# Fused attention and two MLPs: Q and K stored with a head's columns as rows

## The chip, the core and the metric

One NeuronCore of a Trainium2 chip runs the whole program. The metric is device time in microseconds (us) of one execution, given as the median of several. Engines are named as in the profile: PE is TensorE (matmuls; PEld its weight loads), DVE is VectorE, ACT is ScalarE, POOL is GpSimd, SP is SyncE, from whose queue nearly all transfers are issued.

## The reference

Eight batches of eight heads with 576 tokens and 64 columns a head. Keys and values are averaged over groups of 8 tokens (72 pooled rows a head), attention runs over the pooled rows, and its output (4608 tokens x 512) goes through two MLPs one after the other:

```python
k_p = k.reshape(B, H, Sp, pool, D).mean(axis=3)
v_p = v.reshape(B, H, Sp, pool, D).mean(axis=3)
scores = scale * np.matmul(q, k_p.transpose(0, 1, 3, 2))
attn = softmax(scores)
x = np.matmul(attn, v_p)          # then laid out as tokens x 512
h = x @ w_in;  x = (h - np.tanh(h)) @ w_out       # 512 -> 2048 -> 512
h = x @ w2_in; out = (h * np.cos(h)) @ w2_out     # 512 -> 2048 -> 512
```

Q, K and V are 32-bit floats; the MLP weights come as 64-bit floats, which the kernel reads as pairs of 32-bit words and splits into a high and a low part (three matmuls for each product).

## The kernel before, in words

Tokens are worked in blocks of 512 (nine blocks). For each block the first MLP runs 16 steps over slices of 128 hidden columns: `emit_h` (L590, 12 matmuls of 128x512 into PSUM tile `h`), the nonlinearity on ACT and DVE (L600 to L618), and two steps later `emit_out1` (L625, 12 matmuls into `acc`). The second MLP follows (L911 and L990), in an order written out by hand. Block 0 also converts the first MLP's weights as they arrive (`converter`, L173 to L193), blocks 1 to 7 those of the second.

Attention for the tokens of the coming blocks is spread between these steps. It works on tiles of 128 or 96 tokens (five a batch) and is cut into *items*, of which `slot` takes a share ahead of each step; each item's loads are issued `LOOK = 4` items before the item itself. For a batch:

- `load_k` (L260) brings K as five chunks of 128 pooled rows (the last has 64), each row with its 8 tokens of 64 columns; `pool_kv` adds them up on DVE in three halving steps (L291, L291, L292) into `kp`; for batch 0 it is one reduction (L287). ACT doubles the sums (L295).
- `kprep`, in two parts of three and two chunks, transposes `kp` on PE (L325) and lets ACT copy the result into `bd`, a block diagonal of two heads a chunk: 128 rows (two heads' columns) by 144 (two heads' pooled rows), by L332, L336 and L341.
- `load_q` (L346) brings a tile of Q with tokens as rows, in pieces of 64 numbers; `s1` transposes it on PE (L355, four a tile) and ACT copies it to `qT` (L357).
- `s2` multiplies `qT` by `bd` (L371, four matmuls in two halves), takes the maxima (L374), subtracts (L378) and exponentiates (L380); `norm` sums and divides (L385 to L388); `s3` transposes the weights (L400, L410); `pv` multiplies by the pooled V (L433) and writes the MLP's input (L436, L440).

V goes the same way as before and after the change. Up to the first `emit_h` (L1089 to L1188) the order is written out by hand under `manual_schedule`, with `spin` (L1141) for dummy transpositions; there V is summed on POOL. In blocks 0 to 7 the framework's scheduler may reorder what the program lists; from block 8 on the listed order holds. `att_tile` hands out the PSUM tiles of the attention, two in turn.

Of the kernel before, what the change touches and what calls it, by code (L numbers as in the profile page):

```python
# [8 lines left out]
F32 = mybir.dt.float32  # L9
# [31 lines left out]
def fused_kernel(ctx: ExitStack, tc: tile.TileContext, q, k, v, w1i, w1o, w2i, w2o, out):  # L41
    nc = tc.nc
    B, H, S, D = q.shape
    NT, DM = out.shape
    DFF = w1i.shape[1]
# [12 lines left out]
    NKC = (H * SP + 127) // 128  # L58
# [83 lines left out]
    def src_of(wi, wo, f, s):  # L142
        if s == 0:
            return wi.bitcast(U32)[:, f * 256:(f + 1) * 256].rearrange("(c p) n -> p c n", p=128)
        return wo.bitcast(U32)[f * 128:(f + 1) * 128, :]

    def raw_load(src, pool=None, tag="raw"):
        raw = (pool or ap).tile([128, 1024], U32, tag=tag, name="raw", bufs=2)
        nc.sync.dma_start(out=raw.rearrange("p (c n) -> p c n", c=KC) if len(src.shape) == 3 else raw, in_=src)
        return raw  # L150
# [72 lines left out]
    kp = ap.tile([128, NKC, 128], F32, name="kp")  # L223
# [3 lines left out]
    bd = ap.tile([128, NP, 2 * SP], F32, name="bd")  # L227
# [9 lines left out]
    KSPLIT = ((0, 3), (3, NKC))  # L237
# [19 lines left out]
    def load_k(b, c, pool=None, tag="kv", bufs=4):  # L257
        n = min(128, H * SP - c * 128)
        t = slab(tag) if tag in PLACES else (pool or ap).tile([128, POOL * D], F32, tag=tag, name="kv", bufs=bufs)
        nc.sync.dma_start(out=t[:n], in_=k[b].rearrange("h (s r) d -> (h s) (r d)", r=POOL)[c * 128:c * 128 + n, :])  # L260
        raw_kv["k", b, c] = t

    def load_v(b, c, pool=None, tag="kv", bufs=4):
        t = slab(tag) if tag in PLACES else (pool or ap).tile([128, POOL * D], F32, tag=tag, name="kv", bufs=bufs)
# [11 lines left out]
    def pool_kv(which, b, c):  # L276
        t = raw_kv.pop((which, b, c))
        if which == "k":
            n = min(128, H * SP - c * 128)
            o = kp[:n, c, 0:D]  # L280
        elif c < NP:
# [4 lines left out]
        if b == 0 and which == "k":  # L286
            nc.vector.tensor_reduce(o, t[:n].rearrange("p (r d) -> p d r", r=POOL), axis=AX.X, op=ALU.add)  # L287
        else:
            engine = nc.vector if b else nc.gpsimd
            for w in (POOL * D // 2, POOL * D // 4):  # L290
                engine.tensor_tensor(t[:n, :w], t[:n, :w], t[:n, w:2 * w], op=ALU.add)  # L291
            engine.tensor_tensor(o, t[:n, :D], t[:n, D:2 * D], op=ALU.add)  # L292
        if which == "k" and (c == NKC - 1 or (b == 0 and c == KSPLIT[0][1] - 1)):
            c0 = (KSPLIT[1][0] if c == NKC - 1 else 0) if b == 0 else 0
            nc.scalar.activation(out=kp[:, c0:c + 1, D:2 * D], in_=kp[:, c0:c + 1, 0:D], func=AF.Copy)  # L295
# [23 lines left out]
    def kprep(part):  # L319
        c0, c1 = KSPLIT[part]  # L320
        at = att_tile()
        lo, hi = c0 * 128, min(c1 * 128, H * SP)
        for c in range(c0, c1):
            n = min(128, H * SP - c * 128)
            nc.tensor.transpose(at[:, (c - c0) * 128:(c - c0) * 128 + n], kp[:n, c, :], ident[:n, :n])  # L325
        for e in range(2):
            p = e * D
            whole = [h for h in range(e, H, 2) if h * SP >= lo and (h + 1) * SP <= hi]
            m = len(whole)
            x = whole[0] * SP - lo if m else 0  # L330
            if m > 1:
                nc.scalar.activation(  # L332
                    out=bd[p:p + D, whole[0] // 2:whole[0] // 2 + m, e * SP:(e + 1) * SP],
                    in_=at[p:p + D, x:x + 2 * m * SP].rearrange("p (m t) -> p m t", m=m)[:, :, 0:SP], func=AF.Copy)
            elif m:
                nc.scalar.activation(out=bd[p:p + D, whole[0] // 2, e * SP:(e + 1) * SP], in_=at[p:p + D, x:x + SP], func=AF.Copy)  # L336
            for h in range(e, H, 2):
                x0, x1 = max(h * SP, lo), min((h + 1) * SP, hi)
                if h not in whole and x0 < x1:
                    o = e * SP + x0 - h * SP  # L340
                    nc.scalar.activation(out=bd[p:p + D, h // 2, o:o + x1 - x0], in_=at[p:p + D, x0 - lo:x1 - lo], func=AF.Copy)  # L341

    def load_q(t, pool=None, tag="qt", bufs=2, queue=None):
        n = t["n"]
        qt = (pool or ap).tile([128, H * D], F32, tag=tag, name="qt", bufs=bufs)
        (queue or nc.sync).dma_start(  # L346
            out=qt[:n].rearrange("p (h d) -> p h d", h=H),
            in_=q[t["b"], :, t["s"]:t["s"] + n, :].rearrange("h s d -> s h d"))
        t["qt"] = qt

    def s1(t):
        n, qt = t["n"], t.pop("qt")
        at = att_tile()
        for p in range(NP):
            nc.tensor.transpose(at[:, p * 128:p * 128 + n], qt[:n, p * 128:(p + 1) * 128], ident[:n, :n])  # L355
        qT = ap.tile([128, NP, 128], F32, tag="qT", name="qT", bufs=2)
        nc.scalar.activation(out=qT[:, :, :n], in_=at.rearrange("p (g n) -> p g n", g=NP)[:, :, :n], func=AF.Copy)  # L357
        t["qT"] = qT
# [113 lines left out]
    def start_q(t):  # L472
        item(lambda: s1(t), lambda: load_q(t))
# [7 lines left out]
    item(lambda t=t: s1(t), lambda t=t: load_q(t))  # L481
# [7 lines left out]
    item(lambda: None)
    post_kv("k", 1, 4)  # L490
    item(lambda: kprep(0), apart=True)
    post(lambda t=t: norm(t))
    post_kv("v", 1, 0)
    item(lambda t=t: s3(t, 0))
    post_kv("v", 1, 1)
    item(lambda: kprep(1))
    post_kv("v", 1, 2)
    item(lambda t=t: s3(t, 1))
    post_kv("v", 1, 3)
    start_q(tiles[n1])  # L500
    post_kv("v", 1, 4)
# [18 lines left out]
    for c in range(NKC):  # L520
        item(lambda: None)
        post_kv("k", 2, c)
        post_kv("v", 2, c)
    post_kv("v", 2, 5)
    post(lambda: place_v(2))
    item(lambda: kprep(0))
    item(lambda: kprep(1))
    start_q(tiles[n2])

    for ti in range(n2, len(tiles)):  # L530
        t = tiles[ti]
# [551 lines left out]
    if True:  # L1083
# [5 lines left out]
        with tc.manual_schedule():  # L1089
# [16 lines left out]
            load_q(tiles[2], cp, "xe", 4, nc.scalar)  # L1106
            load_q(tiles[3], cp, "xe", 4, nc.scalar)
# [177 lines left out]
```

## Time and profile before

| what | value |
|---|---|
| median of 3 runs | 1728.77 us (1727.46 to 1730.01) |
| the profiled execution, its own time | 1728.11 us |
| its span, first to last instruction | 1726.3 us |
| PE busy | 1696.8 us (98%) |
| PEld, DVE, ACT, POOL busy | 1450.8, 1448.3, 1158.8, 13.8 us |
| mean granted TensorE clock | 0.996 of full speed |
| moved by DMA | 280.24 MB, mean 162 GB/s |

The profile shows one execution. A group of instructions is given with its line, engine, output and input, count, busy time, mean length, and the idle time of the engine just before it with what ended most of that. Matmuls overlap in time, so a group's busy time is more than the time by which it delays what follows; starts tell that. The span leaves out about 2 us of the execution's own time around it.

### The profile page before, as it was taken

How to read it: one execution, taken by the hardware profiler on the slowest of the kernel's cores; microseconds unless marked ns; L12 is line 12 of the kernel's file. 1: busy time of each engine (PE TensorE's matmuls, PEld its weight loads, DVE VectorE, ACT ScalarE, POOL GpSimd, SP SyncE). 2: the span in 40 equal slices, each digit the busy share in tenths (PEclk: the TensorE clock that was granted, in tenths of full speed). 3: DMA queues.
4: the chain of work that ended last, by engine and by line, in shares of the span. 5: the costliest groups of instructions: out<-in, count | busy, mean ns of one | idle time of the engine just before them, and what ended most of it. 6: DMA issues, size and time to landing. Idle time of an engine off the chain costs nothing.

```text
span 1726.3 us, 24077 instructions
## 1 busy us (share of the span) xinstructions
PE 1696.8 (98%) x8268; PEld 1450.8 (84%) x8268; DVE 1448.3 (84%) x2535; ACT 1158.8 (67%) x1926; POOL 13.8 (1%) x30
## 2 busy tenths in 40 slices
PE   6999999999999999999999999999999999999998
PEld 4767888888888888888888888999999998999997
DVE  7899998879999898888767687887887888888776
ACT  5787767767777776776666565656656666656655
POOL 2000000000000000000000000000000000000000
PEclk9999999999999999999999999999999999999999
DMA  7566545556565654636366663532542632632430
GB/s 241 187 213 231 182 139 173 179 183 203 185 224 175 217 184 149 203 134 197 132 205 233 220 198 97 174 114 86 178 127 70 200 111 79 191 120 78 148 98 37
DMA packets 162105, 280.24 MB, mean 162 GB/s; under 512 B 50112, under 2 KB 69568, under 8 KB 161984
## 3 DMA queue, kind: packets, MB, share of 16 engines
q1 hardware_dynamic: 157824, 277.66, 50.2%
q10 hardware_dynamic: 4160, 1.05, 0.3%
q8 instruction: 66, 1.08, 0.2%
q14 instruction: 55, 0.45, 0.1%
HBM read 228.33 MB, written 50.33 MB: 161 GB/s over the span
## 4 chain that ended last, share of the span: by engine, by line
PE 92%; DVE 3%; ACT 3%; DMA 1%; issue 1%; SPq 0%; ACTq 0%
PE acc L990 22%; PE h L590 22%; PE acc L625 22%; PE ab L911 20%; PE att L433 2%; PE att L371 2%; PE att L400 1%; PE att L355 1%; DMA raw<-in_moe_w_in_dram 1%; PE att L410 0%; DMA kv<-in_k_dram 0%; DVE tmp L956 0%; DVE tmp L955 0%; PE att L325 0%; PE acc L433 0%
## 5 line engine op out<-in xcount | busy, mean ns | idle before, releaser
L990 PE MATMUL acc<-wo,gh 128*128 128x512 f32 x1152 | 356.8, 391 | 0.4 <-ACT gh L974 0.4
L911 PE MATMUL ab<-xh,ws 128*128 128x384 f32 x952 | 258.3, 336 | 2.0 <-DVE hB L925 1.4
L990 PEld LDWEIGHTS acc<-wo,gh 128*128 128x128 f32 x1152 | 214.9, 188 | 41.4 <-ACT gh L974 0.8
L990 PE MATMUL acc<-wo,gl 128*128 128x512 f32 x576 | 226.2, 393 | 0.3 <-DVE gl L978 0.3
L590 PE MATMUL h<-xh,wi 128*128 128x512 f32 x576 | 197.1, 401 | 0.1
L590 PE MATMUL h<-xh,ri 128*128 128x512 f32 x576 | 196.5, 401 | 0.0
L625 PE MATMUL acc<-gh,wo 128*128 128x512 f32 x576 | 179.9, 395 | 4.6 <-ACT gh L617 4.6
L625 PE MATMUL acc<-gh,ro 128*128 128x512 f32 x576 | 178.7, 392 | 1.2 <-ACT gh L617 1.2
L911 PEld LDWEIGHTS ab<-xh,ws 128*128 128x128 f32 x952 | 173.5, 188 | 5.9 <-DVE hB L925 2.1
L606 DVE SCALAR_TENSOR_TENSOR tmp<-tmp,h 128x512 f32<-128x512 f32 x144 | 98.4, 683 | 83.2 <-ACT tmp L601 82.4
L911 PE MATMUL ab<-xl,ws 128*128 128x384 f32 x476 | 159.6, 335 | 0.0
L600 ACT ACTIVATE tmp<-h 128x512 f32<-128x512 f32 x144 | 85.5, 594 | 74.5 <-PE h L590 73.9
L617 ACT ACTIVATE gh<-tmp 128x512 fp32r<-128x512 f32 x144 | 90.9, 631 | 62.1 <-DVE tmp L611 59.8
L625 PEld LDWEIGHTS acc<-gh,wo 128*128 128x128 f32 x576 | 108.4, 189 | 28.3 <-ACT gh L617 6.1
L625 PEld LDWEIGHTS acc<-gh,ro 128*128 128x128 f32 x576 | 108.4, 189 | 24.0 <-ACT gh L617 1.5
L990 PEld LDWEIGHTS acc<-wo,gl 128*128 128x128 f32 x576 | 108.0, 188 | 23.6 <-DVE gl L978 0.8
L590 PEld LDWEIGHTS h<-xh,ri 128*128 128x128 f32 x576 | 108.1, 188 | 22.9 <-DVE ri L178 0.9
L974 ACT ACTIVATE gh<-tmp 128x768 fp32r<-128x768 f32 x96 | 81.3, 847 | 67.8 <-DVE tmp L969 67.8
L590 PEld LDWEIGHTS h<-xh,wi 128*128 128x128 f32 x576 | 108.0, 188 | 22.1 <-DVE wi L178 0.6
L609 ACT ACTIVATE tmp<-tmp,bias_m 128x512 f32<-128x512 f32 x144 | 104.1, 723 | 30.9 <-DVE tmp L606 30.3
L922 ACT ACTIVATE z<-ab 128x384 f32<-128x384 f32 x48 | 23.5, 490 | 143.3 <-PE ab L911 143.3
L611 DVE COPY_PREDICATED tmp<-tmp 128x512 f32<-128x512 uint32 x144 | 108.5, 754 | 8.8 <-ACT tmp L609 0.5
(208 smaller groups left out, 3620.3 us busy)
## 6 DMA issues: line engine op xcount, KB each, us to landing
ws<-s2i SPq DMA_DIRECT2D x294, 256.0 KB, 3.0
ri<-s1i SPq DMA_DIRECT2D x64, 512.0 KB, 3.9
ro<-s1o SPq DMA_DIRECT2D x64, 512.0 KB, 3.6
raw<-in_moe_w_in_dram SPq DMA_DIRECT2D x32, 512.0 KB, 4.1
raw<-in_moe_w_out_dram SPq DMA_DIRECT2D x32, 512.0 KB, 3.5
x1s<-xe SPq DMA_DIRECT2D x36, 256.0 KB, 4.1
wo<-s2o SPq DMA_DIRECT2D x18, 512.0 KB, 5.4
out_dram<-xe SPq DMA_DIRECT2D x36, 256.0 KB, 4.1
```

What stands on the lines that cost most here:

```text
L371: nc.tensor.matmul(out=at[:n, j * 2 * SP:(j + 1) * 2 * SP], lhsT=qT[:, p, :n], rhs=bd[:, p, :], start=True, stop=True)
L433: nc.tensor.matmul(out=at[:, :n], lhsT=x, rhs=y, start=(m == 0), stop=(m == len(prods) - 1))
L590: nc.tensor.matmul(out=h[:, off:off + m], lhsT=wi[:, c, wsel, :], rhs=xt[:, r:r + m], start=(n == 0), stop=(n == 3 * KC - 1))
L600: nc.scalar.activation(out=u, in_=h, func=AF.Square)
L606: nc.vector.scalar_tensor_tensor(w, u, C2, h, op0=ALU.mult, op1=ALU.mult)
L609: nc.scalar.activation(out=u, in_=u, func=AF.Relu, bias=bias_m)
L611: step_end[0] = nc.vector.copy_predicated(w, u.bitcast(U32), th)
L617: nc.scalar.activation(out=gh[:, a:e], in_=w[:, a:e], func=AF.Copy)
L625: nc.tensor.matmul(out=acc[d], lhsT=wo[:, wsel, d * 128:(d + 1) * 128], rhs=gt, start=(f == 0 and n == 0), stop=(f == NF - 1 and n == 2))
L911: nc.tensor.matmul(out=out_, lhsT=w[:, wsel, c, :], rhs=x[:, c], start=(m == 0), stop=(m == 5))
L974: nc.scalar.activation(out=g["g" + which][0], in_=g["r" + which], func=AF.Copy)
L990: nc.tensor.matmul(out=acc[NT2 * "AB".index(which) + t], lhsT=gt[:, o:o + 128], rhs=wo2[f][:, wsel, :], start=(j == 0 and e == 0 and m == ...
```

## The change

NumPy hands over other layouts: Q as (batch, head, column, token), K as (batch, head, column, place in the group of 8, pooled row), and both w_in so that a piece of 128 x 128 x 4 weights lies in whole rows, as w_out's pieces do. The kernel then needs neither transposition:

- `load_q` writes `qT` directly, 128 rows (two heads' columns) of 4 x 128 tokens, three buffers instead of two; `s1` is gone. A tile's load hangs on the item before.
- `load_k` brings four chunks of two heads, 128 rows of 8 x 72; `pool_kv` adds on DVE 288 and 144 columns and then, for each head of the two, 72 columns straight into the block diagonal. There are two block diagonals, for even and odd batches. `kp`, L295 and `kprep` are gone. Batch 0 takes the same way as the rest.
- The items lose `s1` and the two `kprep`s of a batch; K's chunk is posted behind the item that ends the tile before, which has V's chunk too.

```diff
     def src_of(wi, wo, f, s):
         if s == 0:
-            return wi.bitcast(U32)[:, f * 256:(f + 1) * 256].rearrange("(c p) n -> p c n", p=128)
+            return wi[f].bitcast(U32)
...
-    kp = ap.tile([128, NKC, 128], F32, name="kp")
-    bd = ap.tile([128, NP, 2 * SP], F32, name="bd")
+    bd = [ap.tile([128, NP, 2 * SP], F32, name=f"bd{j}") for j in range(2)]
...
+    def load_k(b, c):
+        t = ap.tile([128, POOL * SP], F32, tag="kv", name="kv", bufs=4)
+        nc.sync.dma_start(out=t, in_=k[b, 2 * c:2 * c + 2].rearrange("e d r s -> (e d) (r s)"))
         raw_kv["k", b, c] = t
...
     def pool_kv(which, b, c):
         t = raw_kv.pop((which, b, c))
         if which == "k":
+            for w in (POOL * SP // 2, POOL * SP // 4):
+                nc.vector.tensor_tensor(t[:, :w], t[:, :w], t[:, w:2 * w], op=ALU.add)
+            for e in range(2):
+                p = e * D
+                nc.vector.tensor_tensor(
+                    bd[b % 2][p:p + D, c, e * SP:(e + 1) * SP], t[p:p + D, 0:SP], t[p:p + D, SP:2 * SP], op=ALU.add)
+            return
...
-    def kprep(part):
...
+    def load_q(t, qT=None, queue=None):
         n = t["n"]
+        if qT is None:
+            qT = ap.tile([128, NP, 128], F32, tag="qT", name="qT", bufs=3)
         (queue or nc.sync).dma_start(
+            out=qT[:, :, :n], in_=q[t["b"], :, :, t["s"]:t["s"] + n].rearrange("(p e) d s -> (e d) p s", e=2))
-    def s1(t):
...
         t["qT"] = qT
...
-            nc.tensor.matmul(out=at[:n, j * 2 * SP:(j + 1) * 2 * SP], lhsT=qT[:, p, :n], rhs=bd[:, p, :], start=True, stop=True)
+            nc.tensor.matmul(out=at[:n, j * 2 * SP:(j + 1) * 2 * SP], lhsT=qT[:, p, :n], rhs=bd[t["b"] % 2][:, p, :], start=True, stop=True)
...
     def start_q(t):
-        item(lambda: s1(t), lambda: load_q(t))
+        items[-1]["loads"].append(lambda: load_q(t))
...
             start_q(tiles[ti + 1])
-            if b + 1 < B:
+            if b + 1 < B and ti - n2 - 5 * (b - 2) < NP:
                 post_kv("k", b + 1, ti - n2 - 5 * (b - 2))
         item(lambda t=t: s2(t, 0))
         item(lambda t=t: s2(t, 1))
-        if ti + 1 < len(tiles) and tiles[ti + 1]["b"] != b:
-            item(lambda: kprep(0))
-            item(lambda: kprep(1))
...
-            for c in range(3):
+            for c in range(NP):
                 load_k(0, c)
-            load_k(0, 3, cp, "t0", 2)
-            load_k(0, 4, cp, "t0", 2)
             load_q(tiles[0], queue=nc.scalar)
             load_q(tiles[1], queue=nc.scalar)
...
-            nc.gpsimd.memset(kp, 0.0)
-            nc.gpsimd.memset(bd, 0.0)
+            for t in bd:
+                nc.gpsimd.memset(t, 0.0)
...
-            for c in range(KSPLIT[0][1]):
+            for c in range(NP):
                 pool_kv("k", 0, c)
-            s1(tiles[0])
-            kprep(0)
-            for c in range(KSPLIT[1][0], NKC):
-                pool_kv("k", 0, c)
-            s1(tiles[1])
-            kprep(1)
...
-            s1(tiles[2])
             exps(1)
             w1_tick(1)
-            s1(tiles[3])
...
+        if name == "q":
+            a = a.transpose(0, 1, 3, 2)
+        elif name == "k":
+            b, h, s, d = a.shape
+            a = a.reshape(b, h, s // 8, 8, d).transpose(0, 1, 4, 3, 2)
+        elif name.endswith("w_in"):
+            a = a.reshape(-1, 128, a.shape[1] // 128, 128).transpose(2, 1, 0, 3)
+            a = a.reshape(a.shape[:2] + (-1,))
```

The hand-written lists of items for batches 0 to 2 lose the same steps and keep their order otherwise.

## Rows read from the trace of the kernel before

**Rows 1.** Busy time by stretch; columns: us, each engine busy (instructions), clock, DMA.
```profile
0.00:42.00 42.00, 27.98 (x134) 20.38 (x135) 31.47 (x85) 20.92 (x53) 12.37 (x28) 0.96 0.81 247
42.00:180.00 138.00, 129.40 (x575) 99.00 (x576) 126.42 (x260) 110.34 (x218) 0.00 (x0) 0.96 0.63 208
180.00:820.00 640.00, 639.67 (x3145) 531.73 (x3144) 568.02 (x1191) 461.09 (x905) 1.41 (x2) 1.00 0.56 182
```
**Rows 2.** Groups by line and shape, 180 to 820 us: the transpositions of Q and K.
```profile
L355 PE MATMUL att<-ident,qt 128*128 128x128 f32 x72 | 10.6, 272 | 0.0
...
L355 PE MATMUL att<-ident,qt 96*128 96x96 f32 x48 | 5.9, 245 | 0.0
...
L325 PE MATMUL att<-ident,kp 128*128 128x128 f32 x24 | 4.2, 272 | 0.0
```
**Rows 3.** Timeline of PE (start, us, what): four groups of transpositions and their followers.
```profile
255.37 0.49 PE L355 MATMUL att<-ident,qt 96*128 96x96 f32 x4
255.65 0.48 PE L590 MATMUL h<-xh,ri 128*128 128x512 f32 x1
...
300.57 0.39 PE L625 MATMUL acc<-gl,ro 128*128 128x512 f32 x1
300.80 0.60 PE L355 MATMUL att<-ident,qt 128*128 128x128 f32 x4
301.15 0.48 PE L590 MATMUL h<-xh,wi 128*128 128x512 f32 x1
...
596.74 0.49 PE L325 MATMUL att<-ident,kp 128*128 128x128 f32 x3
596.98 0.48 PE L590 MATMUL h<-xh,ri 128*128 128x512 f32 x1
...
602.53 0.47 PE L325 MATMUL att<-ident,kp 128*128 128x128 f32 x2
602.93 0.55 PE L400 MATMUL att<-ident,eb 96*128 96x96 f32 x4
```
**Rows 4.** Groups by line and shape, 180 to 820 us: the sums of K.
```profile
L291 DVE TENSOR_TENSOR kv<-kv 128x256 f32<-128x256 f32 x40 | 16.2, 417 | 2.0 <-DMA kv<-in_k_dram 1.1 <-DMA kv<-in_v_dram 0.8
...
L291 DVE TENSOR_TENSOR kv<-kv 128x128 f32<-128x128 f32 x40 | 11.1, 281 | 0.3
...
L292 DVE TENSOR_TENSOR kp<-kv 128x64 f32<-128x64 f32 x21 | 4.4, 215 | 0.2
```
**Rows 5.** Waits of SP's own queue: who waited for whom, us in total, times, longest.
```profile
SPq L346 <- PE att L355: 55.5, 21, 6.8
```
**Rows 6.** Timeline of DVE in the hand-ordered beginning.
```profile
7.14 1.01 DVE L287 TENSOR_REDUCE kp<-kv 128x64 f32<-128x512 f32 x1 [0.81 <-DMA kv<-in_k_dram]
8.39 1.97 DVE L287 TENSOR_REDUCE kp<-tmp 128x64 f32<-128x512 f32 x2 [0.24 <-DMA tmp<-in_k_dram]
12.84 0.46 DVE L374 TENSOR_REDUCE mx<-att 128x4 f32<-128x288 f32 x1 [2.48 <-PE att L371]
```
**Rows 7.** Busy time by stretch: most of the beginning, columns as in rows 1.
```profile
12.80:32.00 19.20, 13.41 (x71) 10.91 (x71) 18.42 (x49) 10.12 (x27) 7.95 (x16) 0.91 0.91 294
```
**Rows 8.** DMA queues: ACT's from 0 to 8 us, then SP's from 16 to 28.
```profile
q10 hardware_dynamic: 2081, 0.52, 30.2%
...
q1 hardware_dynamic: 3098, 4.06, 101.8%
```
**Rows 9.** DMA issues from 42 to 180 us: count, size, median us to landing.
```profile
raw<-in_moe_w_in_dram SPq DMA_DIRECT2D x14, 512.0 KB, 4.1
raw<-in_moe_w_out_dram SPq DMA_DIRECT2D x12, 512.0 KB, 3.6
```
**Rows 10.** Timeline of PE in block 0: a stop and matmuls behind it.
```profile
51.62 1.87 PE L625 MATMUL acc<-gh,wo 128*128 128x512 f32 x5 [1.43 <-ACT gh L617]
...
54.57 0.63 PE L625 MATMUL acc<-gl,wo 128*128 128x512 f32 x1
```
**Rows 11.** Busy time by stretch: just behind that stop, columns as in rows 1.
```profile
52.00:56.00 4.00, 4.00 (x12) 3.13 (x11) 4.00 (x8) 2.56 (x8) 0.00 (x0) 0.57 0.00 0
```

More of the change, by code (lines that the diff above doesn't have):

```diff
@@ L42, in fused_kernel @@
     nc = tc.nc
-    B, H, S, D = q.shape
+    B, H, D, S = q.shape
     NT, DM = out.shape
-    DFF = w1i.shape[1]
+    DFF = w1i.shape[0] * 128
     POOL = 8
@@ L255, in fused_kernel @@
     raw_kv = {}
[L257 to L260, printed above, removed]
+    def load_k(b, c):
+        t = ap.tile([128, POOL * SP], F32, tag="kv", name="kv", bufs=4)
+        nc.sync.dma_start(out=t, in_=k[b, 2 * c:2 * c + 2].rearrange("e d r s -> (e d) (r s)"))
         raw_kv["k", b, c] = t
     def load_v(b, c, pool=None, tag="kv", bufs=4):
-        t = slab(tag) if tag in PLACES else (pool or ap).tile([128, POOL * D], F32, tag=tag, name="kv", bufs=bufs)
+        t = slab(tag) if tag in PLACES else (pool or ap).tile([128, POOL * SP], F32, tag=tag, name="kv", bufs=bufs)[:, 0:POOL * D]
         src = v[b].rearrange("h (s r) d -> (h s) (r d)", r=POOL)
@@ L285, in pool_kv @@
             o = vr[:n, c - NP, :]
[L286 to L295, printed above, removed]
+        engine = nc.vector if b else nc.gpsimd
+        for w in (POOL * D // 2, POOL * D // 4):
+            engine.tensor_tensor(t[:n, :w], t[:n, :w], t[:n, w:2 * w], op=ALU.add)
+        engine.tensor_tensor(o, t[:n, :D], t[:n, D:2 * D], op=ALU.add)
     def place_v(b):
@@ L317, in place_v @@
                 nc.vector.scalar_tensor_tensor(z, vr[2 * GR:], w[2 * GR:3 * GR], z.bitcast(F32), op0=ALU.mult, op1=ALU.subtract)
-    def kprep(part):
[L320 to L341, printed above, removed]
@@ L343, in load_q @@
-    def load_q(t, pool=None, tag="qt", bufs=2, queue=None):
+    def load_q(t, qT=None, queue=None):
         n = t["n"]
-        qt = (pool or ap).tile([128, H * D], F32, tag=tag, name="qt", bufs=bufs)
+        if qT is None:
+            qT = ap.tile([128, NP, 128], F32, tag="qT", name="qT", bufs=3)
         (queue or nc.sync).dma_start(
-            out=qt[:n].rearrange("p (h d) -> p h d", h=H),
-            in_=q[t["b"], :, t["s"]:t["s"] + n, :].rearrange("h s d -> s h d"))
-        t["qt"] = qt
@@ L351, in s1 @@
-    def s1(t):
[L352 to L357, printed above, removed]
+            out=qT[:, :, :n], in_=q[t["b"], :, :, t["s"]:t["s"] + n].rearrange("(p e) d s -> (e d) p s", e=2))
@@ L480, in fused_kernel @@
     t = tiles[n0]
-    item(lambda t=t: s1(t), lambda t=t: load_q(t))
+    item(lambda: None)
+    start_q(t)
     post_kv("k", 1, 0)
@@ L486, in fused_kernel @@
     post_kv("k", 1, 2)
+    post(lambda t=t: norm(t))
     item(lambda: None)
     post_kv("k", 1, 3)
[L489 to L492, printed above, removed]
+    item(lambda t=t: s3(t, 0))
     post_kv("v", 1, 0)
-    item(lambda t=t: s3(t, 0))
     post_kv("v", 1, 1)
-    item(lambda: kprep(1))
+    item(lambda t=t: s3(t, 1))
     post_kv("v", 1, 2)
-    item(lambda t=t: s3(t, 1))
     post_kv("v", 1, 3)
     start_q(tiles[n1])
+    item(lambda: None)
     post_kv("v", 1, 4)
@@ L519, in fused_kernel @@
     close(tiles[n2 - 1], False)
-    for c in range(NKC):
+    for c in range(NP):
         item(lambda: None)
@@ L523, in fused_kernel @@
         post_kv("v", 2, c)
+    item(lambda: None)
+    post_kv("v", 2, 4)
     post_kv("v", 2, 5)
     post(lambda: place_v(2))
-    item(lambda: kprep(0))
-    item(lambda: kprep(1))
     start_q(tiles[n2])
@@ L538, in fused_kernel @@
         item(lambda t=t: s2(t, 1))
-        if ti + 1 < len(tiles) and tiles[ti + 1]["b"] != b:
-            item(lambda: kprep(0))
-            item(lambda: kprep(1))
         if ti > n2:
@@ L1105, in fused_kernel @@
                 load_v(0, c, cp, tag, bufs)
-            load_q(tiles[2], cp, "xe", 4, nc.scalar)
-            load_q(tiles[3], cp, "xe", 4, nc.scalar)
+            load_q(tiles[2], cp.tile([128, NP, 128], F32, tag="xe", name="qT", bufs=4), nc.scalar)
+            load_q(tiles[3], cp.tile([128, NP, 128], F32, tag="xe", name="qT", bufs=4), nc.scalar)
             for n in range(1, 6):
                 w1_load(n)
-            nc.gpsimd.memset(kp, 0.0)
-            nc.gpsimd.memset(bd, 0.0)
+            for t in bd:
+                nc.gpsimd.memset(t, 0.0)
             values()
@@ L1125, in fused_kernel @@
             nc.vector.tensor_scalar(mk, mk, 1.0 / POOL, None, op0=ALU.mult)
-            for c in range(KSPLIT[0][1]):
+            for c in range(NP):
                 pool_kv("k", 0, c)
-            s1(tiles[0])
-            kprep(0)
-            for c in range(KSPLIT[1][0], NKC):
-                pool_kv("k", 0, c)
-            s1(tiles[1])
-            kprep(1)
             for c in range(NP + NG):
@@ L1270, with layout @@
     arrays, args = {}, []
+    def layout(name, a):
+        if a.dtype == _np.float64:
+            a = _np.ascontiguousarray(a).view(_np.int64)
+        if name == "q":
[6 more added lines that the diff above has]
+            a = a.reshape(a.shape[:2] + (-1,))
+        return _np.ascontiguousarray(a)
     for name in _INS:
-        a = _np.ascontiguousarray(inputs[name])
-        if a.dtype == _np.float64:
-            a = a.view(_np.int64)
+        a = layout(name, _np.asarray(inputs[name]))
         arrays[f"in_{name}_dram"] = a
```

8 lines of the change are left out of this document (2 added, 6 removed).

## The prediction

> **What bounds the kernel now.** I read the page's busy line first, then the stretches, then single groups. TensorE (PE) is busy nearly all of the span, but a share over the whole says nothing about where an instruction taken from it is worth its length. The stretches do [rows 1]: from 180 to 820 us, blocks 1 to 7 of the first layer, PE is busy 639.7 of 640 us while VectorE works 568 and ScalarE 461. There every PE instruction displaces the next. From 42 to 180 us (block 0, whose weights are still being converted) PE has 8.6 us of idle time and a granted clock of 0.96, and VectorE is busy 126.4 of 138 us: two engines share that stretch. Up to 42 us, the hand-ordered beginning, PE is busy 28 us and waits for others. What comes after 820 us holds no instruction that the change touches.
>
> **The steady stretch: PE gives time back.** Removed are the Q transpositions (L355) and the K transpositions (L325). There are 72 + 48 and 24 (with six shorter ones, 30) in the stretch [rows 2]. Their busy time, 10.6 + 5.9 + 4.2 us, is not what they cost, since matmuls overlap; what counts is the time from a group's start to the start of what follows [rows 3]. Four 128-wide Q transpositions take 301.15 - 300.80 = 0.35 us, four 96-wide ones 255.65 - 255.37 = 0.28, the three of a batch's first K part 596.98 - 596.74 = 0.24, the two of its second part 602.93 - 602.53 = 0.40. With 72/4 = 18 groups, 48/4 = 12 groups and six batches: 18 x 0.35 + 12 x 0.28 + 6 x 0.64 = 6.3 + 3.4 + 3.8 = 13.5 us. I take 13.5. The bound above is 14.5, where some of PE's short waits for the Q copy go too. The bound below is 8, where VectorE's fuller stretches give part of it back (below).
>
> **What VectorE gets.** A K chunk cost 417 + 281 + 215 ns [rows 4], and there were five in a batch: 4.6 us. Now there are four chunks of 288, 144 and twice 72 columns. The rows give (417 - 281)/128 = 1.06 ns a column, so 451 + 298 + 2 x 224 = 1.2 us a chunk (the two halves on 64 partitions each priced as a whole instruction), 4.8 us a batch: 0.2 us more, 1.5 us over seven batches. In the steady stretch this lies under PE: 568 + 1.3 over 640 - 13.5 is 91%, against 89%. That cover would go if PE shrank by 70 us. ScalarE loses the Q copies, the doubling of K's sums and the copies into the block diagonal; it is busy 461 of 640 us, so this ends no wait that I can find and has no term.
>
> **Queues.** Q's load now fills its tile directly and has three buffers. SP waited 55.5 us in 21 waits for PE to free a Q buffer [rows 5], with weight and K, V loads queued behind. The new load needs the buffer that the scores of three tiles before have left, which is earlier in the program than the point of issue, so these waits should shrink; since PE waits for no transfer in the steady stretch, I give this nothing there, and no loss either, because a Q load has several items of lead and the same bytes. K's and V's chunks keep their number of bytes and move to one item.
>
> **The beginning.** VectorE's stream of score work starts at 12.84 us, after 2.48 us of waiting for PE [rows 6]; its last K sums end at 8.39 + 1.97 = 10.36. Between lie a ScalarE copy, two transpositions, ScalarE's copies into the block diagonal and the scores. After the change K's sums write the block diagonal. The bytes of K are the same (1.18 MB); the row shows the fourth chunk's reduce waiting for its transfer until 8.39 us. I take this as the landing of the new last chunk, add its 1.2 us of sums, and the maxima start at 9.6, as the first half's scores need only the first two chunks: 3.2 us sooner. VectorE is busy 18.4 of the 19.2 us from 12.8 to 32 us [rows 7], so what follows moves with it. Bounds: 0 if the third tile's Q or V's chunks then end the wait, 4.5 if all of K lands by 7.1, when the third chunk did [rows 6]. ScalarE's Q copies leave this chain too.
>
> Q's transfers compete with K's here. The ScalarE queue moved 2081 packets in 30.2% of 16 engines over 8 us [rows 8], 38.7 us / 2081 = 18.6 ns for a packet of 250 B on average. The SP queue's 3098 packets of 4.06 MB took 101.8% over 12 us, 63 ns for 1,310 B each: 13.5 bytes a ns against 20.8. Q's pieces get longer (64 numbers to 128 or 96). No row has a packet of that length, so the term stands at 3.2.
> The Trainium skill, page "DMA: Bandwidth & Descriptors", section Specifications, says that a transfer needs at least 512 B for line rate; the two queues' rows agree with it. By this rule the first two Q tiles (0.52 MB) would need 1.6 us of all engines, not 2.4, the term would be 4.0 and the forecast 0.8 us lower, while 96-token pieces of 384 B would still miss the mark.
>
> **Block 0.** PE has five transpositions of K, six groups of Q's there, about 2 + 1 us of displacement by the lengths above. Also w_in arrives in whole rows like w_out: 4.1 us to landing against 3.6 [rows 9], 14 loads, some of which ScalarE waits for. VectorE is the fuller engine there and gets no lighter, so I take 2 us, with bounds of 1 us lost (its 0.2 us more and a worse order by the scheduler) and 5 gained.
>
> **Sum.** 13.5 + 2 + 3.2 = 18.7 us. The profiled execution took 1728.11 us (span 1726.3); the median of the runs is 1728.77, 0.7 above. 1728.1 - 18.7 = 1709.4, put at 1710.0 for the median.
>
> **Rivals.**
> *VectorE paces more than I think.* Between 42 and 180 us it is already busy 92% [rows 1]. If block 0 gives nothing and VectorE returns half of the steady gain, 3.2 + 6 = 9.2 remain: 1719.5. For it speaks that K's sums and V's now follow one another; against it that VectorE idles 72 us of the steady stretch. Chance 0.17.
> *Block 0 was waiting for w_in.* If each of 14 loads being 0.5 us sooner shows in full, block 0 gives 7 to 8 us, not 2: 1704. For it: a whole engine queue waits behind a late piece. Against: VectorE's 92%. Chance 0.13.
> *Slower: VectorE in bunches makes PE stop and cool.* Four times a batch a K chunk (1.2 us) and a V chunk (0.9) now come behind one item. Should the step's own VectorE work be late by that, PE stops before the second product. One such stop stands in the trace: 1.43 us idle at 51.62, then matmuls of 0.63 us (54.57) where the same line takes 0.39 at 300.57 [rows 3, 10], the granted clock 0.57 from 52 to 56 us [rows 11], so most of that stretch at 1.2 GHz instead of 2.4. Some 8 matmuls x 0.24 + 1.4 = 3.3 us a stop. Of 28 chunks six would eat the 18.7 us, seven or more make it slower; ten would give 1710 + 33 = 1743. Against it: PE has no stop at all from 180 to 820 us. Chance 0.06.
> The Trainium skill, page "TensorE: Matmul & The Clock Gate", section "What's actually happening", says that the slow clock is the default and activity lifts it, so fewer transpositions mean less to keep it up; the trace agrees at 51.62 us, after an idle PE.
>
> That the change does not do what it says is no rival: the instructions are gone from PE's program.
>
> **How the numbers follow.** The forecast has the rest, 0.64. Least gain of the terms: 0 - 1 + 8 = 7, 1722; most: 4.5 + 5 + 14.5 = 24, 1705, and the w_in case lies at 1704. The range from 1703 to 1722 holds the forecast and most of the first two rivals. A measurement here can tell 0.2%, 3.5 us, from no change. Slower is the third rival, 0.06; within 0.2% is the worst end of the first, 0.03; faster the rest, 0.91.
>
> **What would show it.** In the changed profile: no transposition but those of the attention weights (L400 and L410) and the dummy ones; VectorE's first maximum near 9.6 us; the first L590 near 38.6 us instead of 41.8; the end of block 0 some 5 us sooner; PE still without idle time from there to the second layer, and that stretch 13 to 14 us shorter; after it every stage as long as before. Wrong would be: PE idle before second products in the steady stretch, VectorE above 97% in it, or a first maximum still at 12 us with a transfer as its releaser.

## The result, and the profile after

The changed kernel takes 1714.23 us (median of 4 runs, 1709.06 to 1715.44) against 1728.88 for the kernel before (1727.46 to 1730.01): a ratio of 0.991 with an interval from 0.9888 to 0.9932. It is faster by 14.7 us, not by the 18.7 forecast. The profiled execution took 1713.87 us with a span of 1712.1, 14.2 less than before.

A profile is one execution, and those of one kernel differ by some us. In one set of 13 executions of the kernel before, the time went from 1724.53 us at a mean granted clock of 0.999 to 1731.88 us at 0.995; the profile of the kernel before has 0.996, that of the changed kernel 0.990. A difference of one or two us between two profiles therefore shows nothing by itself.

Busy time by stretch of the changed kernel, columns as in [rows 1]:

```profile
0.00:42.00 42.00, 27.01 (x94) 19.39 (x94) 29.19 (x89) 15.21 (x35) 12.78 (x28) 0.76 0.69 233
42.00:180.00 138.00, 127.19 (x544) 96.62 (x543) 123.71 (x251) 103.70 (x203) 0.00 (x0) 0.95 0.59 201
180.00:820.00 640.00, 639.81 (x3084) 533.59 (x3083) 584.63 (x1236) 447.47 (x858) 1.41 (x2) 1.00 0.56 187
```

From 180 us on PE has no idle time to speak of and VectorE is busy 584.6 / 640 = 91%, as forecast. The first row is the odd one: the granted clock of the first 42 us is 0.76, against 0.96 before. Since the stages themselves shift, stretches with fixed ends cannot be compared. So I cut by events: the first product of the first MLP (L590 before, L547 after), and the starts of the copies that empty block 0 and block 6 (L632 before, L589 after). The timeline of the kernel before has them here:

```profile
41.83 0.50 PE L590 MATMUL h<-xh,wi 128*128 128x512 f32 x1
...
176.47 1.08 ACT L632 ACTIVATE xe<-acc 128x512 f32<-128x512 f32 x2
...
794.28 0.59 ACT L632 ACTIVATE xe<-acc 128x512 f32<-128x512 f32 x1
```

The timeline of the changed kernel has them here:

```profile
46.84 0.50 PE L547 MATMUL h<-xh,wi 128*128 128x512 f32 x1
...
181.72 0.57 ACT L589 ACTIVATE xe<-acc 128x512 f32<-128x512 f32 x1
...
780.66 0.60 ACT L589 ACTIVATE xe<-acc 128x512 f32<-128x512 f32 x1
```

The differences give four stages:

| stage | before | after | difference | forecast |
|---|---|---|---|---|
| beginning, to the first product | 41.8 | 46.8 | +5.0 | -3.2 |
| block 0 | 134.6 | 134.9 | +0.2 | -2 |
| blocks 1 to 6 | 617.8 | 598.9 | -18.9 | -13.5 |
| the rest of the span | 932.0 | 931.4 | -0.6 | 0 |

The stretch from 180 to 820 us that the prediction calls blocks 1 to 7 is blocks 1 to 6 and the beginning of block 7; all 150 transpositions removed from it lie in blocks 1 to 6, so its 13.5 us is set beside that stage.

The sum is -14.2. The total came near the forecast because wrong terms partly cancelled, which is luck: the beginning was forecast 8.2 us and block 0 2.2 us too hopefully, the steady blocks 5.4 us too timidly.

**The beginning.** The first steps went as forecast. The timeline of VectorE in the changed kernel shows the first maximum at 9.80 us, forecast 9.6, before 12.84 [rows 6]; and then a wait that was not foreseen:

```profile
9.80 0.46 DVE L336 TENSOR_REDUCE mx<-att 128x4 f32<-128x288 f32 x1
...
18.30 0.74 DVE L347 TENSOR_REDUCE sm<-eb 128x8 f32<-128x576 f32 x1
22.90 0.46 DVE L276 TENSOR_TENSOR kv<-kv 128x288 f32<-128x288 f32 x1 [3.87 <-DMA kv<-in_k_dram]
23.28 0.17 DVE L348 TENSOR_SCALAR sm<-sm 128x8 f32<-128x8 f32 x1
```

L276 at 22.90 is the first sum of batch 1's keys. The program lists it in block 0, and the scheduler moved it up between the sum (L347) and the division (L348 to L350) of the second tile's weights. It waits 3.87 us for its transfer; the division stands behind it on VectorE, and PE's transposition of these weights needs the division, so both come late. ScalarE does the same with a moved-up step of the weight conversion:

```profile
25.81 0.66 ACT L182 ACTIVATE raw<-raw 128x512 uint32<-128x512 uint32 x1 [4.19 <-DMA raw<-in_moe_w_in_dram]
```

Both steps stood in the beginning before the change as well. There the conversion waited 2.25 us, and the sums, at 23.90, waited for nothing; the timelines of ScalarE and VectorE in the kernel before:

```profile
26.66 0.67 ACT L183 ACTIVATE raw<-raw 128x512 uint32<-128x512 uint32 x1 [2.25 <-DMA raw<-in_moe_w_in_dram]
...
23.90 1.16 DVE L291 TENSOR_TENSOR kv<-kv 128x256 f32<-128x256 f32 x4
```

Neither transfer came later than before: K's was issued at 16.87 us and took 6.0 to land, before the change 17.02 and 6.2, and the conversion went on at 25.81 us instead of 26.66. The DMA engines were full at that time in both kernels; SP's queue from 16 to 24 us (packets, MB, share of 16 engines), before and then after:

```profile
q1 hardware_dynamic: 2193, 2.78, 102.5%
```

```profile
q1 hardware_dynamic: 1533, 3.11, 101.4%
```

VectorE now ran 3 us ahead of a stream of transfers that came 0.3 to 0.9 us sooner, and had to wait for it. What the wait then did to PE is in PE's timeline of the changed kernel:

```profile
24.85 0.63 PE L362 MATMUL acc<-ident,eb 128*128 128x128 f32 x4 [2.25 <-DVE eb L350]
...
27.93 1.19 PE L395 MATMUL acc<-ah,vbd 128*128 128x256 f32 x2 [2.14 <-ACT vbd L302]
29.06 1.22 PE L395 MATMUL acc<-ar,vbr 32*128 32x256 f32 x2
30.20 1.22 PE L395 MATMUL h<-ah,vbd 128*128 128x256 f32 x2
31.36 1.22 PE L395 MATMUL h<-ar,vbr 32*128 32x256 f32 x2
```

and the same products in the kernel before:

```profile
28.74 0.67 PE L433 MATMUL att<-ah,vbd 128*128 128x256 f32 x2 [1.83 <-issue]
29.34 0.69 PE L433 MATMUL att<-ar,vbr 32*128 32x256 f32 x2
29.96 0.70 PE L433 MATMUL acc<-ah,vbd 128*128 128x256 f32 x2
```

PE reaches the products with V 0.8 us sooner than before, but a pair of them takes 1.13 to 1.16 us from start to start instead of 0.60 to 0.62. The stretches of 4 us say why (changed kernel, columns as in [rows 1]; the clock is the third number from the end):

```profile
24.00:28.00 4.00, 1.01 (x7) 0.68 (x7) 3.94 (x12) 2.19 (x7) 0.00 (x0) 0.68 0.88 285
28.00:32.00 4.00, 4.00 (x8) 1.90 (x8) 3.87 (x12) 2.01 (x7) 0.00 (x0) 0.50 0.53 149
32.00:36.00 4.00, 4.00 (x9) 1.54 (x7) 2.74 (x10) 1.32 (x3) 0.00 (x0) 0.50 0.16 52
36.00:40.00 4.00, 4.00 (x17) 3.10 (x17) 0.67 (x2) 2.07 (x5) 0.00 (x0) 0.50 0.02 4
```

PE is busy only 1.01 us of the four from 24 to 28, and for the 12 us behind that it runs at 0.50 of full speed, 1.2 GHz instead of 2.4. In the kernel before it was busy 2.91 us of the same four, and the clock was back at 1.00 from 28 us on:

```profile
24.00:28.00 4.00, 2.91 (x21) 2.61 (x19) 3.96 (x13) 1.75 (x5) 0.00 (x0) 0.86 1.01 321
28.00:32.00 4.00, 3.26 (x11) 1.63 (x12) 3.80 (x14) 3.42 (x12) 0.00 (x0) 1.00 0.49 114
```

**The other terms in the profile after.** The sums of K cost what was worked out from [rows 4]: 298 ns was forecast for 144 columns, 451 for 288 and 224 for 72. Groups by line and shape of the changed kernel, 180 to 820 us:

```profile
L276 DVE TENSOR_TENSOR kv<-kv 128x288 f32<-128x288 f32 x22 | 9.9, 452 | 0.0
L279 DVE TENSOR_TENSOR bd<-kv 64x72 f32<-64x72 f32 x44 | 9.8, 223 | 0.5
...
L276 DVE TENSOR_TENSOR kv<-kv 128x144 f32<-128x144 f32 x22 | 6.6, 298 | 0.1
```

SP's wait for a Q buffer hardly shrank from the 55.5 us of [rows 5] (waits of SP's queue in the changed kernel), and PE still waits for no transfer from 180 to 820 us:

```profile
SPq L318 <- PE att L333: 47.2, 21, 8.2
```

The w_in pieces land sooner, by 0.2 us where 0.5 was thought; w_out's, whose layout is the same, gained 0.4 beside them [rows 9]. DMA issues of the changed kernel, 42 to 180 us:

```profile
raw<-in_moe_w_in_dram SPq DMA_DIRECT2D x14, 512.0 KB, 3.9
raw<-in_moe_w_out_dram SPq DMA_DIRECT2D x12, 512.0 KB, 3.2
```

In block 0 PE waits for ScalarE's copy before second products, 10.7 us in the changed kernel (first fence) and 5.9 in the kernel before (second fence), by the waits of PE from 42 to 180 us:

```profile
PE acc L582 <- ACT gh L574: 10.7, 9, 2.6
```

```profile
PE acc L625 <- ACT gh L617: 5.9, 5, 1.8
```

### The profile page after: what moved, and what is told of

Read it like the earlier page. It is cut to its first block, busy times and chain, and to the rows that moved or that the text cites. A ratio compares the mean times of both kernels' runs of the same rounds, so it can differ in the third digit from the quotient of the medians.

```text
span 1712.1 us, 23572 instructions
## 1 busy us (share of the span) xinstructions
PE 1679.7 (98%) x8068; PEld 1437.7 (84%) x8068; DVE 1448.0 (85%) x2553; ACT 1123.1 (66%) x1829; POOL 14.2 (1%) x30
## 4 chain that ended last, share of the span: by engine, by line
PE 90%; DVE 4%; DMA 2%; ACT 2%; issue 1%; SPq 0%; ACTq 0%; DVEq 0%
PE acc L947 22%; PE h L547 21%; PE acc L582 21%; PE ab L868 20%; PE att L395 2%; DMA raw<-in_moe_w_in_dram 2%; PE att L333 2%; PE att L362 1%; PE att L372 0%; PE acc L395 0%; DMA kv<-in_k_dram 0%; PE h L395 0%; DVE tmp L913 0%; DVE tmp L912 0%; ACT gh L574 0%
## 5 line engine op out<-in xcount | busy, mean ns | idle before, releaser
L547 PE MATMUL h<-xh,wi 128*128 128x512 f32 x576 | 195.4, 399 | 0.1
L547 PE MATMUL h<-xh,ri 128*128 128x512 f32 x576 | 194.6, 398 | 0.0
L547 PEld LDWEIGHTS h<-xh,wi 128*128 128x128 f32 x576 | 108.2, 188 | 22.9 <-ACT wi L192 1.0
L547 PEld LDWEIGHTS h<-xh,ri 128*128 128x128 f32 x576 | 108.1, 188 | 22.0 <-issue 0.3
```

Of the source, the lines that this page charges most:

```text
L547: nc.tensor.matmul(out=h[:, off:off + m], lhsT=wi[:, c, wsel, :], rhs=xt[:, r:r + m], start=(n == 0), stop=(n == 3 * KC - 1))
```

## The experiments

Theory: the moved-up steps that wait for transfers leave PE idle, PE's clock falls to half for the products with V, and that is the lost beginning. Rivals: VectorE's or ScalarE's wait alone costs it and the clock is a bystander; the removed transpositions themselves were what kept the clock up; or part of the change is bad in itself. All stages below (us) were cut as above, from one profile of each kernel; the ratios, with 95% intervals, are to the kernel before, run on the same chip.

| kernel | first product | block 0 | blocks 1 to 6 | span | median | ratio |
|---|---|---|---|---|---|---|
| before | 41.8 | 134.6 | 617.8 | 1726.3 | 1728.88 | |
| after | 46.8 | 134.9 | 598.9 | 1712.1 | 1714.23 | 0.991 (0.9888 to 0.9932) |
| e1_hold_k | 47.2 | 139.9 | 598.8 | 1717.3 | 1719.46 | 0.9955 (0.9941 to 0.997) |
| e2_hold_both | 37.3 | 140.5 | 598.7 | 1707.9 | 1709.30 | 0.9897 (0.9882 to 0.9911) |
| e3_spin | 41.7 | 129.8 | 598.6 | 1701.5 | 1704.57 | 0.987 (0.9855 to 0.9885) |
| e4_hold_spin | 36.7 | 138.5 | 598.7 | 1705.2 | 1707.69 | 0.9889 (0.9872 to 0.9905) |
| e5_spin_act | 42.4 | 129.6 | 598.8 | 1702.3 | 1704.92 | 0.9873 (0.9854 to 0.9893) |
| e6_win_only | 41.3 | 132.3 | 617.9 | 1723.6 | 1724.32 | 0.9985 (0.9976 to 0.9995) |
| e7_old_spots | 46.5 | 135.7 | 598.6 | 1712.3 | 1712.32 | 0.9908 (0.9883 to 0.9933) |
| e8_q_only | 40.7 | 132.4 | 603.6 | 1708.5 | 1710.15 | 0.9904 (0.9882 to 0.9926) |
| e10_k_early | 45.3 | 130.7 | 598.6 | 1706.0 | 1705.10 | 0.9872 (0.9852 to 0.9892) |
| e11_k_early_alone | 44.7 | 129.5 | 599.1 | 1704.6 | 1706.05 | 0.9884 (0.9865 to 0.9903) |

**Holding the moved-up steps: e1_hold_k, then e2_hold_both.** Batch 1's K sums may be issued only behind the last split of the beginning (`first_x`); in e2 the weight conversions also wait for ScalarE's last copy of the beginning.

```diff
+        if which == "k" and b == 1 and not held[0]:
+            raw_kv[which, b, c] = t
+            with tc.issue_after(behind[0].ins):
+                held[0] = True
+                pool_kv(which, b, c)
+                held[0] = False
+            return
...
-        with tc.issue_after(first_x.ins):
+        with tc.issue_after(first_x.ins), tc.issue_after(first_h.ins):
             w1_until(0)
```

> The changed kernel with the sums of batch 1's K held on VectorE behind the beginning's last instruction; nothing else. Theory A (the hoisted sum that waits 3.87 us for its transfer made the beginning late, and PE cooled behind it): no wait of VectorE for K between 19 and 23 us, the granted clock back near 1.0 from 28 to 40 us, the first matmul into h at 41 to 43 us instead of 46.8. Theory B (PE has too little to do without the transpositions, whatever VectorE does): clock still about 0.5 from 28 to 40 us and that matmul at 44.5 us or later. Against the changed kernel's 1714.2 us: A 1709 to 1712 (the 4.8 us of sums now lie in block 0, where VectorE is full, and may give some back), B 1713 to 1716.

> As the run before, and the weight conversions that are listed after the beginning are held on ScalarE too (among them the one that waited 4.19 us for its piece until 25.81 us). Theory A extended: ScalarE's copies for the second tile no longer stand behind that wait, so the first matmul into h comes at 38.5 to 40.5 us, and 1707 to 1711 us in all. Theory B: still 44 us or later. If that conversion was hidden behind VectorE's chain anyway: as the run before, within 1 us.

With the K sums held, VectorE's wait of 3.87 us is gone, yet the first product comes at 47.2 us. ScalarE's wait for its w_in piece is still there, now 4.6 us, and PE does nothing at all from 24 to 28 us. Theory B's numbers for the beginning came, but e2 (below) shows another reason than too little work. The total, 1719.46 us, is outside both ranges: by the ratios this kernel is slower than the changed one. Stretches of e1:

```profile
24.00:28.00 4.00, 0.00 (x0) 0.00 (x0) 0.96 (x2) 1.37 (x4) 0.00 (x0) 0.66 0.94 311
28.00:32.00 4.00, 3.25 (x6) 1.50 (x6) 1.43 (x4) 2.82 (x10) 0.00 (x0) 0.50 0.01 2
```

With both held, both waits are gone, the clock is at 1.00 from 24 to 52 us, and the first product comes at 37.3 us, 9.5 sooner than in the changed kernel, 4.5 sooner than before the change and 1.2 sooner than the earliest expected. Stretches of e2:

```profile
24.00:28.00 4.00, 3.37 (x11) 1.74 (x12) 2.42 (x6) 2.97 (x10) 0.00 (x0) 1.00 0.96 328
28.00:32.00 4.00, 4.00 (x26) 2.74 (x25) 1.93 (x6) 2.40 (x6) 0.00 (x0) 1.00 0.08 22
```

So ScalarE's wait by itself is enough to lose the beginning (VectorE's alone, without more dummies, was not tried), and with neither the layout does shorten it, by what the forecast's upper bound allowed (4.5). But the work held back falls into block 0, which becomes 5 us longer both times: e2 gains 9.5 and returns 5.6. Its ratio is not told apart from the changed kernel's.

**Keeping PE busy through the waits: e3_spin, e4_hold_spin, e5_spin_act.** 38 more dummy transpositions are put where PE idles in the changed kernel; e4 adds e2's holds, e5 only the hold on the conversions.

```diff
             norm(tiles[0])
+            spin(14)
             done(s3(tiles[0], 0))
...
-            spin(8)
+            spin(20)
             done(s3(tiles[1], 0))
             done(s3(tiles[1], 1))
             place_v(0)
             exps(3)
             norm(tiles[2])
+            spin(12)
```

> The changed kernel with 38 more dummy transpositions on PE (14 before the first tile's attention weights, 12 more after the fourth tile's scores, 12 before the products with V), no hold. Theory A: the 3.87 us wait of VectorE stays, so the products with V start at about 28 us as now, but at full clock (0.63 us a pair of matmuls instead of 1.15); 8 pairs and the transpositions beside them give 4 to 5 us, the first matmul into h at 42 to 43 us, 1709 to 1711 us. Theory B: the same start and the same gain, as the missing work is put back; what tells them apart is the run with the hold. If PE's clock in the beginning is worth nothing: 46 to 47 us and 1714.

> Both holds and the dummy transpositions. Theory A: the clock already stays up with the holds, so the dummies add nothing or cost up to 1 us: first matmul into h at 38.5 to 41 us, 1707 to 1711 us, within 1.5 us of the run with both holds. Theory B: at least 3 us faster than the run with both holds.

> The changed kernel with the 38 dummy transpositions and with the weight conversions held on ScalarE behind the beginning, but K's sums left where the scheduler puts them. Theory A (the sums belong in VectorE's gaps of the beginning; held back they cost block 0 about what they took, 4.8 us): first matmul into h at 38 to 41 us, block 0 as short as in the run with dummies alone, 1700 to 1704 us. Theory B (the held conversions are what lengthens block 0, not K's sums): the beginning ends as early, but block 0 takes back 4 us or more as in the run with both holds, 1704 to 1708 us.

In e3 both waits stay (3.8 us on VectorE, 4.1 on ScalarE), but the clock does not fall to half for long; stretches of e3:

```profile
24.00:28.00 4.00, 3.19 (x19) 3.11 (x20) 3.94 (x11) 2.30 (x7) 0.00 (x0) 0.70 0.86 280
28.00:32.00 4.00, 4.00 (x13) 1.80 (x12) 3.87 (x14) 2.84 (x8) 0.00 (x0) 0.87 0.49 139
32.00:36.00 4.00, 2.98 (x18) 1.92 (x18) 3.96 (x14) 2.25 (x6) 0.00 (x0) 1.00 0.50 158
```

The first product comes at 41.7 us: with the waits standing, the clock was worth 5.1 us, and what is left of the beginning is as long as before the change, since VectorE's gain of 3 us goes into the wait. Block 0 is 5.1 us shorter too, which was not expected (1709 to 1711 us in all): 1704.57 us, faster than both kernels (the ratio's interval lies just below that of the changed kernel). With the holds as well (e4) the first product comes at 36.7 us, so the dummies add only 0.6 us where nothing waits, and the waits without the clock cost 5.0 us; but block 0 takes 138.5. With only the conversions held (e5) block 0 stays at 129.6, so it is the held K sums that lengthen it; and the beginning is no shorter than in e3 (42.4 us where 38 to 41 was expected): VectorE's wait remains, 4.56 us there.

**Dummies where the removed transpositions stood: e7_old_spots.** 21 dummies in the changed kernel: 13 behind K's sums, 4 behind the second tile's scores and 4 ahead of the third's.

```diff
             for c in range(NP):
                 pool_kv("k", 0, c)
+            spin(13)
...
             scored(1)
+            spin(4)
             exps(1)
             w1_tick(1)
+            spin(4)
             scored(2)
```

> The changed kernel with 21 dummy transpositions at the places of the beginning from which 16 transpositions of Q and 5 of K were removed (13 before the first scores, 4 and 4 later). If the work that PE lost there is by itself what let its clock fall: granted clock near 1.0 from 28 to 40 us, first matmul into h at 41 to 43 us, 1704 to 1709 us. If it is the idle time before the first and second tile's weights, in which these places do not lie: the clock still about 0.5 from 28 to 40 us, 46 us or later, 1712 to 1716 us.

The first product comes at 46.5 us, and the clock is down as it was; stretches of e7:

```profile
24.00:28.00 4.00, 1.86 (x12) 1.40 (x10) 3.94 (x12) 2.09 (x6) 0.00 (x0) 0.90 0.82 263
28.00:32.00 4.00, 3.96 (x8) 1.82 (x8) 3.88 (x12) 2.11 (x7) 0.00 (x0) 0.53 0.50 144
```

So the second theory came as expected, with 1712.32 us: dummies in the old places do not bring the clock back. That by itself would leave open whether their place or their number (21 against 38) matters; e2 and e11 (below), which have no more dummies than the changed kernel, have the products with V at 1.00 once PE does not idle just ahead of them.

**One part of the change alone: e6_win_only and e8_q_only.** The kernel before with only w_in in whole rows, and with only Q's layout (`s1` left as an empty item).

```diff
-            return wi.bitcast(U32)[:, f * 256:(f + 1) * 256].rearrange("(c p) n -> p c n", p=128)
+            return wi[f].bitcast(U32)
```

```diff
     def s1(t):
-        n, qt = t["n"], t.pop("qt")
...
-        t["qT"] = qT
+        pass
```

> The kernel before with only both w_in laid out in whole rows; Q and K as they were. If block 0 was waiting for its pieces: block 0 shorter by 3 us or more, 1721 to 1725 us. If VectorE paces block 0 anyway (the step of the prediction): within 2 us of the kernel before, 1726 to 1729 us.

> The kernel before with only Q laid out with columns as rows: no L355, no L357, the items kept as empty ones; K and w_in as they were. By the starts in the trace the Q transpositions cost 9.7 us of the 13.5 us from 180 to 820 us. If displacement prices them: blocks 1 to 7 shorter by 9 to 11 us, 1717 to 1722 us in all when the beginning is neither gained nor lost, 1722 to 1727 us when it loses PE's clock as the changed kernel does. If PE's transpositions were filling gaps there: under 4 us shorter.

w_in alone gives 2.3 us in block 0 by the profile, between the two expectations, and 0.15% over all, with an interval from 0.05 to 0.24% (1724.32 us, in the range of the first). Its pieces land 0.4 us sooner (3.7 us in that kernel's DMA issues), but PE idles no less in block 0, 8.9 us against 8.6; what differs there is the granted clock, 0.99 against 0.96. Q alone gives 14.2 of the 18.9 us of blocks 1 to 6, more than the 9 to 11 expected, and leaves the clock of the beginning as it was (0.96, first product at 40.7 us). VectorE's first maximum stands at 13.07 us with Q alone and at 13.12 with w_in alone, so it is K's layout that brought VectorE ahead of its transfers. What K adds in blocks 1 to 6 is 603.6 - 598.9 = 4.7 us, since w_in alone gives nothing there, and it takes more in the beginning; Q alone and the whole change are not told apart by their ratios. K's layout alone was not tried.

**Asking for K earlier: e10_k_early (on e3) and e11_k_early_alone (on the changed kernel).** The first two chunks of batch 1 are requested ahead of the weights.

```diff
+            for c in range(2):
+                load_k(1, c)
             for n in range(1, 6):
                 w1_load(n)
```

> The changed kernel with the 38 more dummy transpositions and with the first two K chunks of batch 1 asked for ahead of the weights in the beginning, so that their sums, which the scheduler moves into the beginning, find their data. Theory A (the moved sums cost the beginning only by their wait of 3.9 us for the transfer, and block 0 is the shorter for having them early): no DVE wait for kv over 1 us between 15 and 30 us, first L590-like product near 39 us instead of 41.7, block 0 still about 130 us, 1701 to 1703 us in all. Theory B (the clock and the dummies decide and the wait of VectorE lies beside them): first product within 0.5 us of 41.7, 1704 to 1706. Theory C (SP's order matters more: the weights behind these two chunks come 1 us later and ScalarE waits the longer): 1706 to 1710.

> The changed kernel with the same two K chunks asked for early and no more dummies. Theory A (VectorE's wait starts PE's idle time, and ScalarE's wait for a piece of w_in keeps it going, as when the sums were held): VectorE's wait at 22.9 us is gone, PE still idles between 24 and 28 us, the granted clock stays at 0.5 behind it, first product at 46 to 47.5 us, block 0 about 134 us as the sums are not held, 1711 to 1715. Theory B (VectorE's wait alone cools PE): clock back at 1.0 by 32 us, first product near 40 us, 1706 to 1708.

Neither theory had this right. With the transfer asked for earlier, the scheduler moved the sums further up, and they wait as long as before, only 8 us sooner; timeline of VectorE in e11:

```profile
14.78 0.46 DVE L277 TENSOR_TENSOR kv<-kv 128x288 f32<-128x288 f32 x1 [4.37 <-DMA kv<-in_k_dram]
```

PE then idles ahead of dummies and transpositions instead of ahead of the products with V, and its clock is back when these come; stretches of e11:

```profile
20.00:24.00 4.00, 0.00 (x0) 0.00 (x0) 3.90 (x12) 0.66 (x1) 1.06 (x3) 0.50 1.03 386
24.00:28.00 4.00, 3.85 (x18) 3.76 (x19) 3.90 (x11) 2.04 (x5) 0.00 (x0) 0.50 0.66 209
28.00:32.00 4.00, 2.62 (x16) 2.33 (x16) 3.87 (x13) 2.24 (x6) 0.00 (x0) 0.79 0.89 261
32.00:36.00 4.00, 3.99 (x13) 2.01 (x14) 3.58 (x12) 3.05 (x10) 0.00 (x0) 1.00 0.29 91
```

So e11's total is what theory B gave, but not for its reason: the wait is still there. Its span is 7.5 us shorter than the changed kernel's, with no more dummies, 2.1 of it in the beginning and 5.4 in block 0; the intervals of the two ratios overlap. On top of the dummies (e10) it brings nothing by the median, 1705.10 against 1704.57. The four executions of e10 lie in two pairs, 1702.4 us at a mean granted clock of 0.998 and 1708 us at 0.995 and 0.996, and its profile, with the first product at 45.3 us, is one of the longer pair; in it PE idles 7.58 us up to 23.83, and the first products with V run at 1.00 all the same.

## Why the prediction was right, and where not

The direction and the main mechanism were right: PE has no slack in the steady blocks, and instructions taken from it come back as time.

**The steady term was mis-sized: 18.9 us, not 13.5, and over its upper bound of 14.5.** I added up the time from each PE record's start to the next one's over blocks 1 to 6:

| PE's work, blocks 1 to 6 | before | Q alone | after |
|---|---|---|---|
| Q transpositions | 10.4 | | |
| K transpositions | 4.1 | 4.0 | |
| products of the first MLP | 535.9 | 533.1 | 533.3 |
| scores | 25.5 | 25.0 | 25.1 |
| transpositions of the weights | 14.5 | 14.2 | 13.6 |
| products with V | 27.1 | 27.0 | 26.9 |

The removed groups themselves took 14.5 us; the step that read a single group of each kind [rows 3] and multiplied was 1 us low. The other 4.4 us lie in what is left, 2.6 of them in the MLP's products and most of the rest in the attention's own work (where six of 168 transpositions of the weights moved to another stage). Nearly all of the 2.6 us is at the seams: a first 512-wide product behind a group of the attention's takes 0.075 us more than its usual 0.227 before the change (120 of them, 9.0 us) and 0.070 after it (108, 7.6 us), and those ahead of a group lose 2.3 and 1.2 us. [rows 3] show it: an L590 right behind a group is 0.48 us long, the L625 ahead of one 0.39. I measured to the start of the follower and left out that the follower is itself longer.

**The beginning was wrong in sign: +5.0 us for -3.2.** The failed step is "VectorE is busy 18.4 of the 19.2 us from 12.8 to 32 us [rows 7], so what follows moves with it". It moved with VectorE only until it met the transfers. The row that tells this stood among those read: SP's queue took 101.8% of 16 engines from 16 to 28 us [rows 8]. It was used for the length of a packet and not for what it says of the stretch, that what needs those bytes does not come sooner while the order of the queue stays (in e11, with another order, the sum's transfer came 8 us sooner). The waits are shown; what they cost through the clock is shown by e3 (5.1 us), and what they cost without it by e3 against e4 (5.0 us). Kernels that share a condition agree on the first product: 46.8 and 46.5 us (changed kernel, e7), 41.7 and 42.4 (e3, e5), 37.3 and 36.7 (e2, e4).

**The third rival had the mechanism, in the wrong place.** It put an idle PE with products at half speed behind it into the steady blocks [rows 10, 11]. There it did not come: the waits of PE from 180 to 820 us are empty. In the beginning it came once, and cost about 5 us. The Trainium skill, page "TensorE: Matmul & The Clock Gate", section "What's actually happening", says that the slow clock is the default and activity lifts it; the fall behind a stretch with PE busy 1.01 of 4.00 us agrees with it, the stay at 0.50 with PE busy 4.00 of 4.00 us from 28 to 40 does not.

**Block 0** gave nothing where 2 us was forecast, within the bounds of 1 us lost to 5 gained. The rival in which it waited for w_in falls: w_in alone gave 2.3 us and not 7 to 8, and PE idled no less (e6). Block 0's length went from 129.5 to 140.5 us over the kernels of the table; held K sums explain the long ones. The others go with the granted clock of the stage: 134.6 to 135.7 us at 0.95 and 0.96 (before, changed kernel, e7), 129.5 to 132.4 us at 0.97 to 0.99 (e3, e5, e6, e8, e10, e11). Of the 5.1 us between the changed kernel and e3, PE's busy time makes 3.1 (124.1 and 121.0 us) and its idle time 2.0 (10.8 and 8.8 us). So the 2 us may have been lost to the clock; why it is lower in one kernel's block 0 than in another's is open.

**VectorE's share and the sums' lengths** came out as forecast, as shown above; SP's waits and w_in's landing shrank less than thought, and no price hung on either in the steady blocks. The rival in which VectorE paces more and takes back half of the steady gain did not come: the steady blocks gave more than forecast.

## What to carry to other kernels

When a change lets an engine run ahead, ask first what it will run into: in a stretch where the DMA queues are full, look up which of its instructions need bytes of that stretch, among them those that a scheduler may move up, since here one of them held up everything behind it. A stop of a few us on another engine can cost as much again through TensorE's clock, here 5.0 us by the stop and 5.1 by the clock; dummies in the very gap repaired it here, fewer dummies elsewhere did not. And a removed group of small matmuls was worth more than its own length: blocks 1 to 6 gave 4.4 us beside the 14.5 of the groups themselves, 2.6 of them in the large products, nearly all at the seams.

## What the runs showed of the hardware that was not expected

A busy PE stayed at its lower clock: from 28 to 40 us the changed kernel shows 4.00 of 4.00 us busy at a granted clock of 0.50, in a row of products with V that ends in transpositions; e1 and e7 show the same from 32 to 40 us. In e2 the same row began at 1.00 and stayed there. In e11 transpositions, dummies and score products ran first at 0.50 and the clock was at 1.00 from 32 to 60 us. What decides between the two was not tried.

Longer pieces help by degrees. In the first 8 us of the changed kernel ScalarE's queue (q10) carries the first tiles of Q, whose pieces are 128 numbers, 512 B, and SP's (q1) mostly K:

```profile
DMA packets 2035, 2.12 MB, mean 265 GB/s; under 512 B 98, under 2 KB 1464, under 8 KB 2035
...
q1 hardware_dynamic: 635, 1.42, 50.1%
q10 hardware_dynamic: 1400, 0.70, 30.1%
```

Between 512 B and 2 KB lie 1464 - 98 = 1366 packets; at 512 B each they are the 0.70 MB of ScalarE's queue. It moved 0.70 MB / (0.301 x 16 x 8 us) = 18.2 bytes a ns of an engine's time, SP's queue in the same 8 us 1.42 MB / (0.501 x 16 x 8 us) = 22.1, with packets of 2,236 B on average, and Q's pieces of 64 numbers before the change 13.5 [rows 8]. The Trainium skill, page "DMA: Bandwidth & Descriptors", section Specifications, asks for at least 512 B for line rate; these packets have just that and reach 18.2 / 22.1 = 82% of the longer ones' rate.
